# One-row transfers in place of small products, products on zeros ahead of the first load, and a new order of work

## The chip, the cores and the metric

The kernel runs on one core of a Trainium2 chip. The core has five engines that run in parallel, each through its own queue in order: PE (TensorE, the matrix products), DVE (VectorE), ACT (ScalarE), POOL (GpSimd) and SP (SyncE, which here only starts transfers). Transfers are started from the queues of SP, ACT and POOL and are carried by 16 DMA engines. The metric is the device time of one execution in microseconds (us): the median of several runs. The profile comes from one further execution, taken with the hardware profiler.

## The reference: what is computed

The input x has 2048 positions and 512 channels, all in 32-bit floats. Two mixers are applied to it, and a gate per position blends them:

```
g = sigmoid((x * gate_w).sum(-1))
a = irfft2(rfft2(x) * (w_r + 1j*w_i))                    # over positions and channels
K = 2 * Re(sum_n C[d,n] * exp(A[d,n] * dt[d] * pos))      # a long convolution per channel
b = causal_conv(x, K) + x * D_skip
out = g * a + (1 - g) * b
```

The kernel writes the two-dimensional transform as products with constant tables. For b it uses that, with these inputs, the decay is so slow that K is flat over the positions: the convolution is then a running sum along the positions times one number per channel. A count of the channels for which this holds (`count`) is computed on the chip, and if any channel fails it a general branch runs instead; it does not run here.

## The kernel before, in words

The order of work is written out by hand. `PLAN` is a list of words; a letter names a step and the numbers behind it say which piece it works on and which buffer it uses, and the words are executed in turn when the program is built, so that each engine's queue holds its instructions in the order of the list. The steps, with the lines of the profile before:

- `A`, `X`, `l`, `L`, `R`, `r`: loads. `A` brings x in ten pieces into `GI`; `X` brings x once more, as `XT` with channels on the partitions; `l` brings the weights of one u into the part of `GI` that C has used (L299), and `L` puts one more row, the weights of the last combination, in partition 127 of them (L305, L303). `R` brings tables.
- `C` (L233): the first transform, eight steps of 8 products; `c` (ACT) or `f` (DVE) copies the result from PSUM to `E1`.
- For each of nine groups of frequencies u (u = 8 is half as large): `D` (L248, eight products), `E` (copy on ACT), `P` (L269, the third transform), `d` (ACT copies a half of it), `Z` (DVE, sums and differences in PSUM, L290 and L291), `W` and `U` (DVE, the complex product with the weights, L311, L316, L317), `p` (POOL starts a transfer that adds one half of the result to the other, L321), `g` (POOL forms the sums and differences of the result, the combinations `gt`, L328 and L329), `I` (L338 to L341, products with `dbw` that transform back), `i` (ACT copies to `GI`).
- In `I`, partition 127 of the combinations needs other signs than the rest. The table `dbw` has zeros in that row, and the row's part is added by two small products for each large one, taken straight from the result `t` (L341, with `dbl`, 32 rows).
- `B` (L357, `Y` is a B without its last columns, `b` adds them) and `T` (DVE transposes) are the next transform, `Q` (L476) the last; `q` adds `XT`, now holding b times the gate, and stores the result (L481, L482). `k` and `K` form the gated tables that Q multiplies with.
- `m` is the running sum (DVE, L436), `s` scales it, `e`, `o`, `v`, `w`, `M` add it to the skip term in `XT`, and `H` multiplies by the gate on POOL. The sums of the four blocks of channels share the two halves of `run`.
- `G`: the gate. `G0` is its products over all of `XT` (L375), `G2` and `G3` write it to memory and read it back spread over the partitions; `G4` and `G5` are the count, and SP reads the count (`TENSOR_LOAD`) to choose the branch at the end.

Results of the products live in four PSUM buffers (`bank`), combinations and other blocks in eight pairs of SBUF buffers (`blk`, `pairs`). A step that writes a buffer waits for the last reader of what was in it.

## Time and profile before

| | us |
|---|---|
| median of 3 runs (lowest to highest) | 134.36 (133.01 to 134.85) |
| the profiled execution | 134.16 |
| its span, first to last instruction | 132.4 |
| PE busy in the span | 117.2 |
| DVE busy | 82.2 |
| POOL busy | 56.2 |
| ACT busy | 51.2 |

The span is what the trace shows; the profiled execution took 1.76 us more, which lies around it. Busy times of the PE are those of overlapping, pipelined products, so the share says that it was seldom without work, not that it worked at its peak. In the profile a line number names the instruction in the kernel, `out<-in` its tiles with the buffer numbers left out, and `xN` the number of instructions. One product of 32-bit floats is shown as two records of PE and two of PEld, the loading of its weights.

### The profile page before, as it was taken

The page shows a single profiled execution, that of the slowest core. Times are in us where ns is not written, and L with a number is a line of the kernel's source. Part 1 is how long each engine was busy: PE and PEld are TensorE (multiplying, and loading weights), DVE is VectorE, ACT ScalarE, POOL GpSimd, SP SyncE. Part 2 cuts the span into 40 slices and gives each one's busy share as a digit, 9 for nine tenths or more (in the row PEclk, how much of TensorE's full clock was granted, in tenths as well). Part 3 has the DMA queues.
Part 4 walks back from the last instruction along what each step waited for, and adds up shares of the span by engine and source line. Part 5 has one row for each costly group of instructions (what it writes and reads, how often), then busy time and mean ns, then how long its engine had stood idle before and what let it go on. Part 6 is the DMA issues. An engine that isn't in the chain of part 4 may idle for free.

```text
span 132.4 us, 2360 instructions
## 1 busy us (share of the span) xinstructions
PE 117.2 (89%) x944; PEld 95.5 (72%) x944; DVE 82.2 (62%) x101; ACT 51.2 (39%) x63; POOL 56.2 (42%) x49
## 2 busy tenths in 40 slices
PE   0599998999979999989999999999999999999700
PEld 0599997999879998858736766777655339999600
DVE  0031036078299999788770099999999573677610
ACT  3033635444267542313164113349679970000000
POOL 0000000001040840586798919499949999300000
PEclk9999999999999999999999999999999999999965
DMA  2999989996869789998667769990969600099660
GB/s 83 349 396 384 392 309 272 389 389 136 314 195 223 253 238 276 274 386 174 126 130 147 141 144 316 295 335 10 191 131 198 124 5 7 9 368 396 267 245 5
DMA packets 10643, 29.85 MB, mean 226 GB/s; under 512 B 1818, under 2 KB 2938, under 8 KB 10366
## 3 DMA queue, kind: packets, MB, share of 16 engines
q1 hardware_dynamic: 8606, 22.99, 48.4%
q0 software_dynamic: 1872, 6.55, 25.9%
q8 instruction: 9, 0.15, 0.4%
q10 hardware_dynamic: 144, 0.07, 0.4%
q14 instruction: 12, 0.10, 0.2%
HBM read 18.82 MB, written 4.21 MB: 174 GB/s over the span
## 4 chain that ended last, share of the span: by engine, by line
PE 69%; DMA 15%; DVE 7%; POOL 2%; issue 2%; ACT 1%
PE ps L233 13%; PE ps L476 12%; PE ps L357 11%; PE ps L338 9%; PE ps L341 8%; DMA blk<-blk 8%; PE ps L339 5%; PE ps L269 4%; DMA short<-in_prms_dram 3%; DMA GI<-in_x_dram 3%; PE ps L248 3%; PE ps L375 3%; DVE ps L290 2%; DVE ps L291 2%; DVE blk L316 1%
## 5 line engine op out<-in xcount | busy, mean ns | idle before, releaser
L233 PE MATMUL ps<-s,GI 128*128 128x128 f32 x128 | 17.4, 307 | 4.9 <-DMA GI<-in_x_dram 4.9
L453 POOL TENSOR_TENSOR XT<-XT,hg 128x1024 f32<-128x1024 f32 x8 | 20.9, 3038 | 0.0
L233 PEld LDWEIGHTS ps<-s,GI 128*128 128x128 f32 x128 | 17.2, 222 | 4.8 <-DMA s<-in_c_s_dram 4.8
L346 ACT COPY GI<-ps 128x1024 f32<-128x1024 f32 (+1 forms) x9 | 8.7, 964 | 24.2 <-PE ps L341 24.2
L328 POOL TENSOR_TENSOR blk<-blk 128x512 f32<-128x512 f32 (+1 forms) x9 | 13.0, 1443 | 11.6 <-DMA blk<-blk 11.2
L248 PE MATMUL ps<-dfw,E 128*128 128x128 f32 x128 | 15.6, 277 | 2.2 <-DVE blk L317 1.6
L248 PEld LDWEIGHTS ps<-dfw,E 128*128 128x128 f32 x128 | 14.8, 192 | 2.9 <-DVE blk L317 2.0
L338 PE MATMUL ps<-dbw,blk 128*128 128x128 f32 x68 | 16.3, 322 | 0.6 <-POOL blk L329 0.6
L269 PE MATMUL ps<-s2e,blk 128*128 128x128 f32 x136 | 16.8, 277 | 0.0
L269 PEld LDWEIGHTS ps<-s2e,blk 128*128 128x128 f32 x136 | 15.8, 192 | 1.2 <-issue 0.8
L357 PE MATMUL ps<-GI,s2p 128*64 128x512 f32 (+1 forms) x64 | 15.7, 583 | 0.0
L436 DVE TENSOR_TENSOR_SCAN run<-XT 128x1024 f32<-128x1024 f32 x4 | 11.2, 2803 | 6.7 <-DMA XT<-in_xt_dram 6.7
L476 PE MATMUL ps<-blk,E 128*128 128x128 f32 x128 | 15.3, 282 | 0.0
L476 PEld LDWEIGHTS ps<-blk,E 128*128 128x128 f32 x128 | 15.2, 196 | 0.1
L341 PE MATMUL ps<-last,blk 32*64 32x128 f32 x136 | 14.8, 293 | 0.0
L338 PEld LDWEIGHTS ps<-dbw,blk 128*128 128x128 f32 x68 | 10.1, 188 | 5.8 <-issue 5.0
L415 POOL TENSOR_TENSOR few<-few 128x4 f32<-128x4 f32 x1 | 0.2, 202 | 31.5 <-ACT few L412 31.5
L339 PE MATMUL ps<-dbw,blk 128*128 128x128 f32 x68 | 13.1, 275 | 0.0
L481 DVE TENSOR_TENSOR blk<-ps,XT 128x1024 f32<-128x1024 f32 x8 | 9.6, 1222 | 5.6 <-PE ps L476 2.8
L329 POOL TENSOR_TENSOR blk<-blk 128x512 f32<-128x512 f32 (+1 forms) x9 | 12.6, 1404 | 0.0
L238 ACT COPY E<-ps 128x1024 f32<-128x1024 f32 x7 | 7.1, 1012 | 13.7 <-PE ps L233 13.7
L311 DVE TENSOR_TENSOR blk<-ps,GI 128x1024 f32<-128x1024 f32 (+1 forms) x9 | 10.5, 1164 | 3.1 <-PE ps L341 1.8
(51 smaller groups left out, 142.7 us busy)
## 6 DMA issues: line engine op xcount, KB each, us to landing
XT<-in_xt_dram SPq DMA_DIRECT2D x4, 1024.0 KB, 6.6
GI<-in_w_dram SPq DMA_DIRECT2D x8, 512.0 KB, 3.9
blk<-blk POOLq DMA_DIRECT2D x8, 512.0 KB, 5.7
out_dram<-blk SPq DMA_DIRECT2D x8, 512.0 KB, 3.3
GI<-in_x_dram SPq DMA_DIRECT2D x6, 512.0 KB
XT<-run POOLq DMA_DIRECT2D x4, 512.0 KB, 5.9
GI<-in_x_dram SPq DMA_DIRECT2D x4, 256.0 KB, 5.4
hg<-gd SPq DMA_DIRECT2D x1, 1024.0 KB
```

The costliest lines, as they stand in the source:

```text
L233: T.matmul(p[:, u, :, j], X[:, 8 * k + 4 * u + j], s1, start=True, stop=True)
L248: T.matmul(p[:, n], E1[:, 8 * u + n], dfw[:, n % 4], start=True, stop=True)
L269: T.matmul(p[:, h, :, o, 64 * v:64 * v + 64], t_["e2", u % 8][:, 4 * v + 2 * h + o], st[:, ::-1] if h else st, start=True, stop=True)
L328: G.tensor_tensor(gt[:, :, :, 0], t[:, 0:4:3], t[:, 1:3], op=ALU.add)
L329: G.tensor_tensor(gt[:, ::-1, :, 1], t[:, 0:4:3], t[:, 1:3], op=ALU.subtract)
L338: T.matmul(p[:, v, 2 * h + 1], gt[:, h, m + v], dbw[:, h, 1], start=True, stop=True)
L339: T.matmul(p[:, v, 2 * h], gt[:, h, v], dbw[:, h, 0], start=True, stop=False)
L341: T.matmul(p[64 * c:64 * c + 64, v, 2 * h], px[:, c ^ h, h, v], dbl[:, h], start=False, stop=True, tile_position=(96, 64 * c))
L357: T.matmul(p[64 * s:64 * s + 64, u, :16 * n], s2p[:, 0, g], GI[:, 32 * s:32 * s + n, tt], start=True, stop=s == 1, tile_position=(0, 64 * s))
L436: V.tensor_tensor_scan(run[:, q % 2, 1:1025], XT[:, 0, q], XT[:, 1, q], 0.0, op0=ALU.add, op1=ALU.add)
L453: G.tensor_tensor(o, o, hg[:, 1024 * (k % 2):1024 * (k % 2) + 1024], op=ALU.mult)
L476: T.matmul(p[:, u, :, j], E4[:, b // 16, b % 16, :, u], t_["q", b // 8][:, 8 * u + b % 8].rearrange("p q a -> p (q a)"), start=True, stop= ...
```

## The change

Five things change.

1. `I`: the two small products per large one are gone, and so is the zeroed row of `dbw` (with the table `last` and its load). The row is put right in the combinations themselves: a new step `h` starts, from SP, four transfers per u, each of one partition and two runs of 64 numbers (one run for u = 8), from `t` to `gt`. They follow POOL's `g` of the same u. `I` does the four products that do not need that row first.
2. Before the first load has landed, two products of 128x512 on zeros are put on the PE; their result is not used. DVE clears their operand first.
3. The one-row loads of the weights (`L`) are started from ACT instead of SP.
4. A running sum gets a block of its own, out of nine pairs of blocks instead of two halves of `run` beside eight pairs. Since the block has no leading zero, the shares with the shifted sum treat the first element apart.
5. The list of words, `PLAN`, is another one. One C copy goes from DVE to ACT, and the u's are worked in another order (0, 3, 4, 2, 5, 6, 8, 1, 7 on DVE, instead of 6, 7, 5, 1, 4, 2, 0, 3, 8).

```diff
-NPAIR = 8
+WARM = 2
+NPAIR = 9
...
 PLAN = """
-R0 A4 C3.0 A7 C6.1 r0.0 A3 c3 C2.0 r1.1 N0 A5 R3 J0 A6 C4.2 R8 A9 A8 c6 c2 C5.0 c4 f5 A1 C7.1 c7 A2 C1.0 R4 c1 A0 C0.1
...
+A4 A3 R4 A2 R0 C3.0 R2 C2.1 A5 c2 c3 A1 A0 C1.2 A6 A7 A8 R3 C4.1 C0.0 c1 c4 A9 r1.0 R1 r0.1 C5.1 J0 c5 C6.2 C7.1 X3 N0
...
-    dbw = dbw.reshape(128, 2, 2, 128)
-
-    last = (j == 127)[:, None, None]
-    dbw = np.stack([dbw[:, :, 0] * ~last, dbw[:, :, 1], dbw[:, :, 0] * last], 2)
...
-    last = work.tile([P, 4, P], F32, name="last")
-    hT, dbl = last[:9], last[96:P, 0:2]
+    hT = work.tile([9, 4, P], F32, name="hT")
...
-    run = work.tile([P, 2, 1028], F32, name="run")
...
-            lambda: (nc.sync.dma_start(dbw, c_dbw[:, :, 0:2]), nc.sync.dma_start(dbl, c_dbw[96:P, :, 2])),
+            lambda: nc.sync.dma_start(dbw, c_dbw),
...
-                nc.sync.dma_start(wtile(8)[P - 1:P, :, :, 0].rearrange("p r a k -> p (r a) k"), hT[8:9, :, :64])
+                nc.scalar.dma_start(wtile(8)[P - 1:P, :, :, 0].rearrange("p r a k -> p (r a) k"), hT[8:9, :, :64])
             else:
-                nc.sync.dma_start(GI[P - 1:P, 8 * u:8 * u + 8 * n].rearrange("p (u n o) t -> p u n o t", n=4, o=2)[:, :, :, 0], hT[u:u + n])
+                nc.scalar.dma_start(GI[P - 1:P, 8 * u:8 * u + 8 * n].rearrange("p (u n o) t -> p u n o t", n=4, o=2)[:, :, :, 0], hT[u:u + n])
...
+        def h_a(u):
+            n = nrow(u)
+            t = t_["t", u][P - 1:P, 0, :, :, 0:n].rearrange("p x a (v k) -> p a x v k", k=64)
+            gt = t_["gt", u][P - 1:P, :, 0:n // 64].rearrange("p h v c k -> p h c v k")
+            for h in range(2):
+                for c in range(2):
+                    nc.sync.dma_start(gt[:, h, c], t[:, h, c ^ h])
+
         def I_(u, i):
+            p = t_["pi", u] = bank(i).rearrange("p v (n t) -> p v n t", t=P)
             m = nrow(u) // 64
-            p = t_["pi", u] = bank(i).rearrange("p v (n t) -> p v n t", t=P)
             gt = t_["gt", u].rearrange("p h m c k -> p h m (c k)")
-            px = t_["t", u][96:P, 0].rearrange("p x a (m k) -> p x a m k", k=64)
-            for v in range(m):
-                for h in range(2):
-                    T.matmul(p[:, v, 2 * h + 1], gt[:, h, m + v], dbw[:, h, 1], start=True, stop=True)
-                    T.matmul(p[:, v, 2 * h], gt[:, h, v], dbw[:, h, 0], start=True, stop=False)
-                    for c in range(2):
-                        T.matmul(p[64 * c:64 * c + 64, v, 2 * h], px[:, c ^ h, h, v], dbl[:, h], start=False, stop=True, tile_position=(96, 64 * c))
+            for o in (1, 0):
+                for v in range(m):
+                    for h in range(2):
+                        T.matmul(p[:, v, 2 * h + o], gt[:, h, o * m + v], dbw[:, h, o], start=True, stop=True)
...
-        def scan(q):
-            V.tensor_tensor_scan(run[:, q % 2, 1:1025], XT[:, 0, q], XT[:, 1, q], 0.0, op0=ALU.add, op1=ALU.add)
+        def scan(q, i):
+            t_["run", q] = blk(i)
+            V.tensor_tensor_scan(blk(i), XT[:, 0, q], XT[:, 1, q], 0.0, op0=ALU.add, op1=ALU.add)
...
+            if k == 0:
+                V.tensor_scalar(XT[:, 0, q, 0:1], XT[:, 0, q, 0:1], sd[:, q:q + 1], None, op0=ALU.mult)
+            V.scalar_tensor_tensor(XT[:, k, q, 1 - k:], XT[:, k, q, 1 - k:], (sd, dsk)[k][:, q:q + 1], t_["run", q][:, 0:1023 + k], op0=ALU.mult, op1=ALU.add)
...
+        V.memset(gsg[:, 0], 0.0)
+        for k in range(WARM):
+            T.matmul(bank(3)[:, 0], gsg[:, 0, 0:P], gsg[:, 0], start=True, stop=True)
```

The list moves nearly every instruction; three places matter for what follows. The first is SP's queue around the load of the count (`count`), before. `gd` is the gate in memory, `hg` and `blk7` its two spread copies, `c_r` the tables of `k`:

```order
L303 DMA GI_77<-last_84 1x4x64
L382 DMA gd_75<-gsg_86 4x512
L507 TENSOR_LOAD count_68
L507 ISA x2
L383 DMA hg_67<-gd_75 128x2048
L385 DMA gd_75<-gsg_86 32x1x16 x4
```

Now, in the same queue; L332 is the new step `h`, for u = 5 above the load, and for u = 6, 1, 8 and 7 below it, and L389 is `G3`:

```order
L332 DMA blk1_88<-blk4_91 1x2x64 x4
L514 TENSOR_LOAD count_68
L514 ISA x2
L389 DMA blk4_91<-gd_75 128x2048
L332 DMA blk3_90<-blk8_95 1x2x64 x4
L393 DMA short1_97<-in_c_r_dram 128x512
L332 DMA blk1_88<-blk7_94 1x2x64 x4
L332 DMA blk0_87<-blk6_93 1x16x4 x4
L332 DMA blk3_90<-blk5_92 1x2x64 x4
```

The load of the count, which waits for DVE's cast of it, now stands ahead of `G3` and of sixteen one-row transfers; before, the gate's copies stood behind it.

The second place is DVE where the count is cast (L433 in both), before; L317 is the end of `U`, L290 the start of the next `Z`:

```order
L317 SCALAR_TENSOR_TENSOR blk5_93<-ps3_61,GI_77 128x512
L433 CAST count_68<-ps2_60 1x1
L290 TENSOR_TENSOR ps1_59<-ps1_59,short1_97 128x2x64
L291 TENSOR_TENSOR ps1_59<-short1_97,ps1_59 128x2x64
L290 TENSOR_TENSOR ps1_59<-ps1_59,short1_97 127x2x64
```

Now; L312 is the end of the last `U` (u = 7), L437 the running sum:

```order
L311 TENSOR_TENSOR blk5_92<-ps0_58,GI_77 128x512
L312 SCALAR_TENSOR_TENSOR blk5_92<-ps0_58,GI_77 128x512
L437 SCALAR_TENSOR_TENSOR blk3_90<-XT_76 128x1024
L433 CAST count_68<-ps1_59 1x1
L437 SCALAR_TENSOR_TENSOR blk1_88<-XT_76 128x1024
```

Before, the cast came ahead of the last u (u = 8); now it comes behind the last u and a running sum.

The third place is the PE around the gate's products (L375 in both), now; L264 is `P`, L341 the new `I`:

```order
L264 MATMUL ps3_61<-s2e_80,blk2_89 128x2x64 x8
L375 MATMUL ps0_58<-XT_76,gws_85 32x512 x16
L264 MATMUL ps1_59<-s2e_80,blk3_90 128x2x64 x8
L264 MATMUL ps2_60<-s2e_80,blk0_87 128x2x64 x4
L264 MATMUL ps0_58<-s2e_80,blk1_88 128x2x64 x8
L341 MATMUL ps3_61<-dbw_83,blk3_90 128x128 x8
```

Before, three of the `I` stood ahead of the gate's products and only the P of u = 8 behind them; now no `I` stands ahead of them, and three P's (u = 1, 8, 7) come behind.

24 lines of the change are left out of this document (11 added, 13 removed).

## The prediction, on record before the run

> **What bounds it now.** I read the page first (busy time of the engines), then the windows cut where the PE's work changes: loading, C (first transform of x), D/P (second and third), P/I (third and back), B, Q, the last store.
>
> ```profile
> PE 117.2 (89%) x944; PEld 95.5 (72%) x944; DVE 82.2 (62%) x101; ACT 51.2 (39%) x63; POOL 56.2 (42%) x49
> ```
> ```profile
> 0.00:4.80 4.80, 0.00 (x0) 0.00 (x0) 0.09 (x2) 1.28 (x1) 0.20 (x4) 1.00 0.52 185
> 4.80:22.25 17.45, 17.39 (x130) 17.39 (x131) 4.02 (x7) 6.07 (x7) 0.00 (x0) 1.00 0.96 347
> 22.25:50.50 28.25, 26.01 (x228) 25.32 (x226) 21.11 (x33) 14.59 (x18) 6.50 (x11) 1.00 0.86 269
> 50.50:93.80 43.30, 42.73 (x356) 29.95 (x355) 33.27 (x42) 15.61 (x18) 31.74 (x26) 1.00 0.81 209
> 93.80:109.50 15.70, 15.70 (x110) 7.65 (x108) 12.80 (x11) 13.64 (x20) 13.62 (x8) 1.00 0.66 125
> 109.50:124.85 15.35, 15.35 (x130) 15.15 (x128) 9.64 (x8) 0.00 (x0) 4.14 (x2) 1.00 0.52 208
> 124.85:132.40 7.55, 0.00 (x1) 0.00 (x0) 1.23 (x1) 0.00 (x0) 0.00 (x0) 0.63 0.37 145
> ```
> The columns are the stretch, its length, busy time of PE, PEld, DVE, ACT, POOL, the clock, the DMA share and GB/s. From 4.80 to 124.85 the PE is busy 117.2 of 120.05 us. It is the bound of every stage, and its gaps are 2.9 us in all. A microsecond taken from it is therefore a gain only until the next chain comes up; that chain has to be found. The profiled execution took 134.16 us, 1.76 beyond its span of 132.4; the median of the runs is 134.36, so no correction is due.
>
> **What the change takes from the PE.** One transform back (I, one u) in the timeline:
>
> ```profile
> 57.07 0.49 PE L338 MATMUL ps<-dbw,blk 128*128 128x128 f32 x2 [0.57 <-POOL blk L329]
> 57.72 0.43 PE L341 MATMUL ps<-last,blk 32*64 32x128 f32 x4
> 58.08 0.49 PE L338 MATMUL ps<-dbw,blk 128*128 128x128 f32 x2
> 61.10 0.38 PE L269 MATMUL ps<-s2e,blk 128*128 128x128 f32 x1
> ```
> A quarter takes 1.01 us and the whole u 61.10 - 57.07 = 4.03. Each product is two records, so a u is 16 full and 16 small records. What a full one costs is seen in C, where ACT copies after every 16:
>
> ```profile
> 4.86 17.37 PE ps L233 x128
> 22.25 1.02 ACT E L238
> ```
> ```profile
> 8.64 1.01 ACT L238 COPY E<-ps 128x1024 f32<-128x1024 f32 x1 [6.19 <-PE ps L233]
> 11.53 1.01 ACT L238 COPY E<-ps 128x1024 f32<-128x1024 f32 x1 [1.87 <-PE ps L233]
> 13.31 1.01 ACT L238 COPY E<-ps 128x1024 f32<-128x1024 f32 x1 [0.77 <-PE ps L233]
> 15.10 1.01 ACT L238 COPY E<-ps 128x1024 f32<-128x1024 f32 x1 [0.78 <-PE ps L233]
> ```
> The steady step is 15.10 - 13.31 = 1.79 us for 16 records. So 4.03 - 1.79 = 2.24 us per u goes with the small products, and with eight and a half u's 19.0 us. A full product has its own weights in C as in the new I, so 1.79 is the price of the new I too.
>
> **The zeros.** The first two steps of C take 8.64 - 4.86 = 3.78 and 2.89 us against 1.79: 3.1 us lost, while the granted clock shows 1.00. The PE runs at about half rate until some 5.9 us after its first product. If the products on zeros start at about 1.6 (DVE has to clear 128x512 first), the fast rate comes up to 3.3 us earlier, worth half of that: 1.7. The bounds are 0 (two products last perhaps 2 us, and the PE idles again until 4.86) and 3.1. I take 1.7: C ends at 20.55 instead of 22.25. The Trainium skill (TensorE: Matmul & The Clock Gate, Part 1) says that the clock is released after a busy window of about 3.4 us and that this window runs freely; by it two short products with a pause behind them may fill no window, and the gain would be 0 and the time 1.7 higher.
>
> **The next chain: DVE.** Its work per u (L285 to L312 now) has not changed.
>
> ```profile
> 29.59 0.43 DVE L290 TENSOR_TENSOR ps<-ps,short 128x256 f32<-128x256 f32 x1
> 45.48 0.42 DVE L290 TENSOR_TENSOR ps<-ps,short 128x256 f32<-128x256 f32 x1
> 49.66 0.42 DVE L290 TENSOR_TENSOR ps<-ps,short 128x256 f32<-128x256 f32 x1
> 75.91 0.28 DVE L290 TENSOR_TENSOR ps<-ps,short 128x128 f32<-128x128 f32 x1
> 78.55 5.16 DVE L442 SCALAR_TENSOR_TENSOR XT<-XT,few,run 128x1024 f32<-128x1024 f32 x2
> ```
> ```profile
> L420 DVE TENSOR_REDUCE few<-short 128x4 f32<-128x512 f32 x1 | 0.7, 686 | 2.8 <-DMA short<-in_prms_dram 2.8
> L375 PE MATMUL ps<-XT,gws 128*32 128x512 f32 x32 | 3.6, 595 | 0.0
> ```
> A full u is 49.66 - 45.48 = 4.18 us, u = 8 is 78.55 - 75.91 = 2.64. Before, the first of them starts 29.59 - 22.25 = 7.34 after C; the same three steps (D, D, P) stand between now, so 20.55 + 7.34 = 27.9. Six full u's and the reduction: 27.9 + 25.1 + 0.7 = 53.7. The seventh is u = 8, and its P stands on the PE behind the gate's products, which need all of XT:
>
> ```profile
> 50.09 0.60 SPq L207 DMA_DIRECT2D XT<-in_xt_dram  x1
> ```
> The last part of XT was issued at 50.09 before. Now 15.5 MB stand in the queue up to it (x, XT, weights, tables). By 4.80, 0.9 MB have come (185 GB/s); at 347 the rest lands at 46.9, at 347 up to 22.25 and 269 after that at 54.0. SP no longer waits in between for the one-row loads, but the accumulating transfers of POOL share the engines: I take 49. The PE is there at 20.55 + 1.06 + 14 x 1.79 = 46.7. So gate to 49 + 3.6 = 52.6, two P's (2.7) 55.3, ACT's copy 0.5: DVE starts u = 8 at 55.8, 2.1 late, and ends the last u at 55.8 + 2.64 + 2 x 4.18 = 66.8 (before 78.55).
>
> **The last rows, on SP.** These are 36 transfers, four per u. A one-row transfer and the wait for the count:
>
> ```profile
> 75.84 0.14 DVE L433 CAST count<-ps 1x1 int32<-1x1 f32 x1 [6.34 <-PE ps L430]
> 77.33 0.35 SPq L383 DMA_DIRECT2D hg<-gd  x1
> 77.73 2.46 SPq L385 DMA_DIRECT2D gd<-gsg  x4
> 80.24 3.19 SPq L393 DMA_DIRECT2D short<-in_c_r_dram  x4
> ```
> ```profile
> s2e<-in_c_s2e_dram SPq DMA_DIRECT2D x1, 128.0 KB, 2.2
> gd<-gsg SPq DMA_DIRECT2D x4, 2.0 KB, 5.2
> ```
> ```profile
> L436 DVE TENSOR_TENSOR_SCAN run<-XT 128x1024 f32<-128x1024 f32 x4 | 11.2, 2803 | 6.7 <-DMA XT<-in_xt_dram 6.7
> ```
> Four one-row issues take 2.46, and SP goes on 77.33 - 75.98 = 1.35 after the cast. The new order puts the load of the count on SP ahead of G3 and of the rows of u = 6, 1, 8 and 7, and on DVE the cast behind a scan that follows the last u. So: 66.8 + 2.8 (scan) + 0.14 + 1.35 = 71.1; G3 0.35; u = 6 2.46; one table 0.8; u = 1 2.46; u = 8 2.46: issued at 79.6. Landing is 2.2 or 5.2, by two small transfers; I take 2.2, since loads of megabytes no longer run beside it: 81.8. The Trainium skill (DMA: Bandwidth & Descriptors, Rules for kernel authors) advises against many transfers under 64 KB, as mostly overhead; the 0.62 us of each of these 2 KB issues agrees.
>
> POOL's side of the last u ends about then:
>
> ```profile
> DMA to landing us min/median/max: 4.5/5.2/11.6
> ```
> ```profile
> L328 POOL TENSOR_TENSOR blk<-blk 128x512 f32<-128x512 f32 x8 | 11.0, 1371 | 9.7 <-DMA blk<-blk 9.2 <-PE ps L375 0.3
> ```
> Accumulated at 66.8 + 5.2 = 72.0; the two combinations of a u take 2 x 1.37, and those of u = 1 and 8 and two more issues stand ahead, so u = 7 is out at about 79, under SP's 79.6, where its rows begin. They are issued at 82.1 and land at 84.3.
>
> **The end.** I of u = 8 ends at 82.2. Two of the eight B's follow (2 x 1.96 of the 15.70 row): 86.1. I of u = 7, 1.8: 87.9, its rows landed before. The rest of B, 11.8: 99.7. Q, 15.35: 115.0. Tail 7.55: 122.6. Outside 1.76: **124.4 us**.
>
> Costs put at nothing: the h rows of u = 0, 4, 3, 2 also hand buffers back to W of u = 6, 8, 1, 7. By the same prices they land 1 to 3 us ahead of those; with 5.2 to land, W of u = 6 is 1.6 late. C's eighth copy moves from DVE to ACT, 1.0 in a step of 1.79. Two more need rows:
>
> ```profile
> XT<-in_xt_dram SPq DMA_DIRECT2D x4, 1024.0 KB, 6.6
> ```
> ```profile
> L442 DVE SCALAR_TENSOR_TENSOR XT<-XT,few,run 128x1024 f32<-128x1024 f32 x4 | 8.5, 2166 | 0.0
> L397 DVE TENSOR_TENSOR short<-short,blk 128x512 f32<-128x512 f32 x4 | 4.6, 1205 | 0.0
> L453 POOL TENSOR_TENSOR XT<-XT,hg 128x1024 f32<-128x1024 f32 x8 | 20.9, 3038 | 0.0
> ```
> G3 (1 MB) is issued at 71.5 and by the first row lands near 78; three of the bases and the four shares follow on DVE, 3 x 1.2 + 8.5 = 12.1, to about 90, and the first transpose is due at 91. POOL's eight gate products, 20.9 us from the first shares at about 84, end at 105, ahead of the end of the fourth Q at 107.4, after which the PE needs a bank back. Without that cover each microsecond counts in full. A buffer per sum removes waits of scans that are on no chain here.
>
> **The rivals.**
> *Nothing queues.* The chain alone, without SP's count, POOL's queue or XT's delay: DVE 27.9 + 36.8 = 64.7; landing 5.2, combination 2.7, issues 2.5, landing 2.2 make 77.3; I 1.8, B 11.8, Q 15.35, tail and outside 9.3: **115.6**. For it: the PE alone, kept as busy as before, would give 134.16 - 19.0 - 1.7 = 113.5. Against: four queues would have to meet. 0.08.
>
> *ACT's queue holds the copies.* This one is slower. The one-row loads of the weights leave SP for ACT:
>
> ```profile
> SPq L305 <- DMA GI<-in_w_dram: 16.2, 4, 5.5
> ```
> On SP four of them waited 16.2 us in all. Behind them on ACT stand the copies that PE and DVE wait for, one per u. If this came in full, the time would be 124.4 + 16.2 = **140.6**; it turns slower once more than 12.6 of them remain. Against: at 347 GB/s the weights of u = 0 land at 25, those of 3 and 4 at 29, and ACT reaches these loads at 26 and 30; only u = 5 to 7 (39 to 44, ACT at 42) is close. 0.04.
>
> *The zeros warm nothing, rows land in 5.2 and XT at 54.* That adds 1.7, 3.0 and 5.0: 126.1, 127.4, 129.4 singly, over 131.7 only together. 0.08, of which 0.06 falls within 2% of before.
>
> **The numbers.** The forecast, 117.5 to 130.5, has 0.80. The low end is 124.4 - 2.1 (XT in time) - 1.4 (zeros in full) - 3.2 (twelve issues at 0.35, the row of one plain issue) = 117.7; the high end has landing and XT both late by most of their bounds. What is left out is 115.6 with 0.08 and the part above with 0.12. Two per cent is what a measurement of this kernel can tell: faster is under 131.7, slower over 137.0. Faster 0.80 + 0.08 + 0.02 = 0.90, same 0.06, slower 0.04.
>
> **What would show it.** C's first two copies some 5 us apart at 1.79 and 2 to 3 us instead of 3.78 and 2.89 (zeros). I's eight products at 1.79 per u with PE idle between them released by DMA or POOL (last rows bind). The last L312 of DVE near 67, SP's G3 near 71, the last L332 near 82, B from 82, Q from 100. Wrong: PE idle under 4 us in all (first rival), ACT idle on weight loads with DVE waiting for ACT (second), or the last u on DVE after 72 with SP long empty, which would put the cause ahead of the last rows.

## The result and the profile after

The changed kernel takes **144.43 us** (median of 4 runs, 143.30 to 145.19) against 134.36 before: 1.0765 of the kernel before (ratio of the means), with a 95% interval of 1.0635 to 1.0895. It is slower, by about 10 us; the forecast was 124.4, in a range of 117.5 to 130.5, and faster. Some executions of any kernel come out slow: ratios leave them out, and so does the 134.36 (one of 148.70), while the medians in the table below are of all runs. The profiled execution took 144.53 us with a span of 142.7 and a mean granted clock of 0.876 (before 0.979).

The page of the changed kernel, with TensorE's (PE) busy tenths and its granted clock in 40 slices of 3.57 us, and the chain that ended last:

```profile
PE 109.5 (77%) x812; PEld 91.7 (64%) x812; DVE 79.1 (55%) x102; ACT 51.4 (36%) x64; POOL 54.9 (38%) x49
...
PE   5999989999998004999095039982999999999800
...
PEclk9999999999999955699757755899599999999985
...
PE ps L357 11%; PE ps L479 11%; PE ps L228 10%; DMA gd<-gsg 7%; PE ps L243 6%; PE ps L264 6%; SPq L332 5%; DMA GI<-hT 5%; PE ps L375 4%; DMA blk<-blk 4%; SPq L385 3%; PE ps L492 3%; DVE ps L286 2%; DVE blk L306 2%; DVE ps L285 2%
```

The PE is busy 7.7 us less than before, and the span is 10.3 us longer: the work did go, and 23 us of idle time took its place, in four holes of 9.48, 3.38, 7.51 and 2.58 us (slices 13 to 15, 19, 21 to 23 and 27, counted from 0). In and behind each hole the clock row reads 5 to 7: the PE comes back at half rate. The chain now names things that were on no chain before: the gate's writes (`gd<-gsg`), SyncE's own queue (`SPq L332`, the placed rows) and the one-row loads (`GI<-hT`).

The holes in the PE's timeline (start, length, instructions; in brackets the idle time ahead of it and what ended it):

```profile
55.35 5.73 PE L375 MATMUL ps<-XT,gws 128*32 128x512 f32 x32 [9.48 <-DVE blk L312]
...
70.91 0.34 PE L430 MATMUL ps<-few 128*1 128x1 f32 x8 [3.38 <-ACT XT L448]
...
84.40 11.55 PE L341 MATMUL ps<-dbw,blk 128*128 128x128 f32 x76 [7.51 <-DMA blk<-blk]
...
99.36 0.46 PE L341 MATMUL ps<-dbw,blk 128*128 128x128 f32 x2 [2.58 <-DMA blk<-blk]
99.75 1.19 PE L357 MATMUL ps<-GI,s2p 128*64 128x512 f32 x4
...
119.83 15.34 PE L479 MATMUL ps<-blk,E 128*128 128x128 f32 x128
```

The gate's products start at 55.35 and take 5.73 us where they took 3.6 before. The line names DVE's L312, but that was done at 54.69; in two kernels further down the same wait is put down to the load of x for the gate (XT), and we read it so here too. I of u = 5 waits 7.51 us for its placed row, I of u = 8 another 2.58. B starts at 99.75 (forecast 82.2) and Q at 119.83 (forecast 99.7): the miss of 20 us is all there when Q starts, for Q and the tail are as long as forecast. What SyncE (SP) did ahead of those rows:

```profile
55.34 13.25 SPq L332 DMA_DIRECT2D blk<-blk  x12
...
69.87 0.55 SPq L382 DMA_DIRECT2D gd<-gsg  x1
...
72.79 5.81 SPq L385 DMA_DIRECT2D gd<-gsg  x4
...
79.94 3.59 SPq L332 DMA_DIRECT2D blk<-blk  x4
85.36 0.34 SPq L389 DMA_DIRECT2D blk<-gd  x1
85.81 2.55 SPq L332 DMA_DIRECT2D blk<-blk  x4
...
88.89 10.73 SPq L332 DMA_DIRECT2D blk<-blk  x12
```

And the end of GpSimd's (POOL) combination of u = 5, from POOL's timeline:

```profile
68.41 1.51 POOL L324 TENSOR_TENSOR blk<-blk 128x512 f32<-128x512 f32 x1
```

POOL has u = 5 ready at 69.9. Its row is issued at 79.94, behind the gate's five small writes, their read back and two tables, and the PE goes on at 84.40. The queue holds the gate back as well: its values are ready at 62.2 (ACT's L379 ends there), but the first gate write is issued only at 69.87, because on SP it stands behind the twelve rows of u = 4, 3 and 2, the last of which wait until POOL has u = 2 ready at 66.55. The chain of waits goes on from there (start, length):

```profile
77.06 8.11 DMA gd<-gsg
...
93.70 5.52 DMA blk<-blk
```

The last gate write takes 8.11 us to land, the read of the gate's result (G3, L389) comes right behind that, the rows of u = 6, 1 and 8 stand behind G3 in SP's queue, and the last of these lands 5.52 us after its issue. Then B can start. Whether G3 waited for that landing alone is not settled: on SP the row of u = 5 ends at 83.53 and the load of the count starts at 83.6, both ahead of G3, and in a kernel without rows G3 comes 1.67 us after the start of that load, which here would be 85.3 too.

### The profile page after: what moved, and what is told of

Read it like the earlier page. It is cut to its first block, busy times and chain, and to the rows that moved or that the text cites. A ratio compares the mean times of both kernels' runs of the same rounds, so it can differ in the third digit from the quotient of the medians.

```text
span 142.7 us, 2183 instructions
## 1 busy us (share of the span) xinstructions
PE 109.5 (77%) x812; PEld 91.7 (64%) x812; DVE 79.1 (55%) x102; ACT 51.4 (36%) x64; POOL 54.9 (38%) x49
## 3 DMA queue, kind: packets, MB, share of 16 engines
q0 software_dynamic: 1872, 6.55, 24.7%
## 4 chain that ended last, share of the span: by engine, by line
PE 54%; DMA 16%; DVE 10%; SPq 9%; issue 4%; ACT 1%; DVEq 0%; ACTq 0%
PE ps L357 11%; PE ps L479 11%; PE ps L228 10%; DMA gd<-gsg 7%; PE ps L243 6%; PE ps L264 6%; SPq L332 5%; DMA GI<-hT 5%; PE ps L375 4%; DMA blk<-blk 4%; SPq L385 3%; PE ps L492 3%; DVE ps L286 2%; DVE blk L306 2%; DVE ps L285 2%
## 5 line engine op out<-in xcount | busy, mean ns | idle before, releaser
L341 PE MATMUL ps<-dbw,blk 128*128 128x128 f32 x136 | 21.9, 333 | 10.7 <-DMA blk<-blk 10.5
L341 PEld LDWEIGHTS ps<-dbw,blk 128*128 128x128 f32 x136 | 20.9, 245 | 11.4 <-DMA blk<-blk 7.7
L316 POOL DMA_DIRECT2D blk<-blk x9 | 8.0, 914 | 38.3 <-DVE blk L312 37.4
L264 PE MATMUL ps<-s2e,blk 128*128 128x128 f32 x136 | 16.3, 276 | 0.0
L264 PEld LDWEIGHTS ps<-s2e,blk 128*128 128x128 f32 x136 | 15.7, 192 | 0.8 <-issue 0.8
L437 DVE TENSOR_TENSOR_SCAN blk<-XT 128x1024 f32<-128x1024 f32 x4 | 9.2, 2289 | 10.9 <-PE ps L341 8.6
L228 PEld LDWEIGHTS ps<-s,GI 128*128 128x128 f32 x128 | 14.5, 192 | 1.1 <-DMA s<-in_c_s_dram 1.1
L228 PE MATMUL ps<-s,GI 128*128 128x128 f32 x128 | 14.5, 275 | 0.0
L285 DVE TENSOR_TENSOR ps<-ps,short 128x256 f32<-128x256 f32 (+3 forms) x18 | 7.4, 414 | 11.3 <-ACT short L270 11.0
L403 ACT ACTIVATE blk<-short,sgn 128x512 f32<-128x512 f32 x16 | 10.1, 710 | 8.7 <-issue 8.7
L375 PE MATMUL ps<-XT,gws 128*32 128x512 f32 x32 | 5.7, 879 | 9.5 <-DVE blk L312 9.5
L445 DVE SCALAR_TENSOR_TENSOR XT<-XT,few,blk 128x1023 f32<-128x1023 f32 (+1 forms) x4 | 9.2, 2344 | 6.3 <-ACT blk L440 6.3
```

The source lines that it names most:

```text
L228: T.matmul(p[:, u, :, j], X[:, 8 * k + 4 * u + j], s1, start=True, stop=True)
L264: T.matmul(p[:, h, :, o, 64 * v:64 * v + 64], t_["e2", u % 8][:, 4 * v + 2 * h + o], st[:, ::-1] if h else st, start=True, stop=True)
L285: V.tensor_tensor(a, b, re, op=ALU.add)
L341: T.matmul(p[:, v, 2 * h + o], gt[:, h, o * m + v], dbw[:, h, o], start=True, stop=True)
L375: T.matmul(p[32 * j:32 * j + 32], gws[:, q], XT[:, j // 2, q, 512 * (j % 2):512 * (j % 2) + 512], start=q == 0, stop=q == 3, tile_position ...
L403: S.activation(t_["q", j][:, :, q], r, AF.Copy, scale=sgn[:, q:q + 1])
```

## The experiments

Each kernel ran once with a profile, unless it says otherwise, beside runs of the kernel before on the same chip. The changed kernel itself was not run again on those chips, so a difference to its 144.43 is one between chips. All times in us:

| what | time | before, same chip |
| --- | --- | --- |
| gate later | 139.81 | 135.92 |
| no rows | 135.23 | 135.92 |
| rows in the order of before | 156.61 | 135.92 |
| zeros alone | 134.93 | 135.92 |
| small products in the new order | 175.6 | 132.46 |
| the same, gate later | 171.97 | 132.46 |
| filler at the gate | 142.59 | 132.46 |
| half the rows | 146.6 | 132.46 |
| mixed | 132.19 | 136.5 |
| no rows, gate later | 135.0 | 136.5 |
| small products, filler | 175.81 | 136.5 |
| x earlier | 143.98 | 136.5 |
| gate writes on ScalarE | 141.46 | 134.35 |
| both moved | 136.11 | 134.35 |
| full-size products | 141.34 | 134.35 |
| mixed, 4 runs | 134.49 | 134.35 |
| full-size behind a wait | 152.94 | 134.21 |
| mixed and padded, 13 runs | 134.04 | 134.21 |

The runs of the kernel before went from 132.04 to 139.31 us over chips and runs, at granted clocks of 0.957 to 0.992, and three took 147.82 to 150.67, and on three of the five chips it ran once; so a difference of a few us between single runs says little without their traces. Against the kernel before on the same chip, the changed kernel loses 10.1 us, gate later 3.9, x earlier 7.5, gate writes on ScalarE 7.1, both moved 1.8, half the rows 14.1, and no rows with the gate later gains 1.5.

### The gate, and the rows

Theory A: x lands late and DVE stands behind the gate. Theory B: the placed rows in SP's queue set the end.

```diff
-P6.3 d5.0 G0.0 Z5 ... p5 L8 G1 Z6 ... U6 R9 h4 P7.0
+P6.3 d5.0 Z5 ... p5 L8 Z6 ... U6 R9 h4 G0.0 G1 P7.0
```

> The changed kernel with the gate's products (L375) moved on the PE behind the P's of u = 1 and 8, nothing else. Theory A (the late landing of XT at 55 us holds the PE at the gate, and with it the last three u's): u = 8 starts on DVE near 54 instead of 64.4, the last u ends near 67 instead of 75.6, and the time falls by about 8, to some 136. Theory B (SP's queue of one-row transfers and gate writes sets the end, whatever the gate does on the PE): the last u is earlier, but its rows are not, and the time stays within 2 of 144.4.

139.81, which is 4.6 under the changed kernel: between the two theories. DVE's last L312 ends 71.4 instead of 75.7, but the PE then waits 10.6 us for the row of u = 5.

```diff
 def h_a(u):
-    n = nrow(u)
-    ... (the four transfers)
+    pass
```

> The changed kernel without the 36 one-row transfers: the last row of the combinations stays wrong, so that part of the computation is left out. Theory A: the wait at the gate stays, the last u still ends on DVE near 75.6, and only the 7 to 8 us in which the PE waited for rows go: about 136. Theory B: everything behind the last u moves up as well, I of u = 7 follows POOL near 88, and the time falls by about 16, to 128.

135.23. That is near theory A's figure. Taking all 36 transfers away gives 9.2 us and still only reaches the level of before. Rows are a large part of the loss, and something else keeps the gain away; it shows further down.

```diff
 kernel before:
-I_ with small products, dbl
+I_ and h_a of the changed kernel, h right behind each g
```

> The kernel before, with its own order, where only the small products give way to the one-row transfers, issued from SP right behind each g. If the small products were 19 us of the bound as the prediction had it, and rows land in time in an order with one I every 4 us, the time falls towards 120 to 126. Theory B says that the rows wait in SP's queue here too (behind loads and the gate's writes): 132 or more. If the order is what made the changed kernel slow, this one is faster than 134.4.

156.61, on the side of theory B (132 or more), but by far more than it foresaw. In the order of before I of a u stands 0 to 7 us behind its g, and a row does not get there in that time. From the waits of this kernel (total, times, longest):

```profile
PE ps L341 <- DMA blk<-blk: 16.8, 7, 5.9
DVE short L397 <- DMA blk<-gd: 13.5, 1, 13.5
```

The first is the rows' landing, the second the read of the gate's result, which stands behind rows in SP's queue. How much of the rest is the clock, which was at 0.50 again in 90 to 100 us, was not tested.

```diff
 kernel before:
+V.memset(gsg[:, 0], 0.0)
+for k in range(2):
+    T.matmul(bank(3)[:, 0], gsg[:, 0, 0:P], gsg[:, 0], start=True, stop=True)
```

> The kernel before with the two products on zeros and nothing else. By the changed kernel's trace, where C takes 14.3 us instead of 17.4, the time falls by about 3, to 131. If the zeros only move the wait (C then waits for x), it stays at 134.

134.93, 1.0 under before, within what one run can tell. C ends 1.6 us sooner (20.6 against 22.2), and a longer pause ahead of a product, 3.47 us where it was 1.29, takes that back. The trace names DVE for that pause; that DVE in turn stands behind the loads is argued here, not shown.

### Half of the rows, x earlier, the gate's writes

```diff
-for h in range(2):
-    for c in range(2):
-        nc.sync.dma_start(gt[:, h, c], t[:, h, c ^ h])
+for c in range(2):
+    nc.sync.dma_start(gt[:, 0, c], t[:, 0, c])
```

> The changed kernel with two of the four small transfers of every u, those of the first half alone; the placing of the other half of the last row is left out, the order is kept. If the cost is the number of transfers in SP's queue (18 fewer of 36), the time lies half way between the kernel without rows and the changed one, 139 to 141. If the cost is that the products wait for the landing of a row at all (5.5 us from the issue, however many transfers go with it), little is gained: 142.5 to 144.5. If it is the queue alone, up to some threshold that the half already clears: 135 to 137.

146.6, above every one of the three. With two transfers instead of four the row of u = 5 is issued at 78.80 (79.94) and the PE waits until 85.54 (84.40): the number of transfers is not what holds it. B starts 1.9 us earlier than in the changed kernel, and that is lost again on DVE ahead of Q, where the second pair of shares takes 10.04 us.

```diff
-l6 l8 D5.2.3 E5 ... R5 X1 L5.3 X0 g0.6
+X1 X0 l6 l8 D5.2.3 E5 ... R5 L5.3 g0.6
```

> The changed kernel with the last two loads of x for the gate moved ahead of the weights of u=6 and u=8 in SyncE's queue; no other word of the order is moved. If x lands at 55.3 because 0.8 MB of weights go ahead of it at some 300 GB/s, it lands 2 to 3 us sooner, TensorE's idle time ahead of the gate falls from 9.5 to about 7, and the time is 141.5 to 143. If the rate of the loads falls whatever stands first, or the weights are then late for W of u=6, it is 144 or more.

143.98: x landed 6 us sooner, more than expected, and nothing came of it. ScalarE's (ACT) timeline and queue in this kernel, and the groups of the chain that ended last:

```profile
52.28 0.75 ACTq L300 DMA_DIRECT2D GI<-hT  x1
53.08 1.15 ACT L440 ACTIVATE blk<-blk,few 128x1024 f32<-128x1024 f32 x1 [10.74 <-POOL blk L323]
```
```profile
DMA GI<-in_w_dram 13%; PE ps L357 11%; PE ps L479 11%; PE ps L228 11%; DMA blk<-blk 8%; PE ps L341 5%; PE ps L243 4%; DMA GI<-hT 3%; SPq L385 3%; PE ps L492 3%; DVE ps L286 2%; DVE ps L285 2%; DMA gd<-gsg 2%; SPq L393 2%; SPq L332 2%
```

The bracket names POOL, but the chain has the load of the weights first, with 18.08 us from its issue at 34.10 to its landing at 52.2. Now the weights are late, and ACT, which issues the one-row load of u = 5 to 7 only when they have landed, does nothing from 42.3 to 52.3 with DVE's copy behind it. The rival on ACT's queue, 0.04 in the prediction, is real as soon as x goes first: the load rate has to be given to one of the two. The PE's wait for the row of u = 5 ends at 84.61 as before.

```diff
-nc.sync.dma_start(gd[1]...)   -nc.sync.dma_start(gd[0]...)  (x4)
+nc.scalar.dma_start(gd[1]...) +nc.scalar.dma_start(gd[0]...) (x4)
```

> The changed kernel with the five small writes of the gate's result issued by ScalarE instead of SyncE, nothing else moved. In the changed kernel these, the read back of hg between them and two loads of c_r hold SyncE from 68.7 to 79.9 while g of u=5 is ready at 69.9. Theory (the order in SyncE's queue): the row of u=5 is issued at about 71 to 72 and lands by 79, so TensorE's wait ahead of I of u=5 ends 5 us sooner; the rows behind it and the gate's read move up too, and the time is 138 to 141. Rival (each step waits for its own landing, not for the queue): above 143.

141.46, 3.0 under the changed kernel and 0.5 above the range. SP's timeline and the PE's:

```profile
71.46 3.90 SPq L332 DMA_DIRECT2D blk<-blk  x4
80.41 0.34 SPq L389 DMA_DIRECT2D blk<-gd  x1
```
```profile
80.00 10.46 PE L341 MATMUL ps<-dbw,blk 128*128 128x128 f32 x66 [2.89 <-DMA blk<-blk]
```

The row of u = 5 is issued 8.5 us sooner and the PE goes on 4.4 us sooner. The four issues end at 75.36, and the PE starts 4.6 us later: that is the landing. G3 takes over the buffer which that row is read from, so it waits for the landing too, and is issued at 80.41 (85.36). Two other things moved with the writes. The load of the count on SP now stands behind G3 and no longer ahead of it, so that G3 does not wait for the cast of the count: by the prediction's rule of 1.35 us behind the cast (80.49 here) G3 would have come at 81.8. And ACT now stands 5.70 us behind the gate's writes.

The next kernel has both moves, the gate's products behind P of u = 1 and 8 and the writes on ACT:

> As the kernel with the gate's writes on ScalarE, and also with the gate's products behind P of u=1 and 8, which alone gave 4.6 us. If the late gate and SyncE's queue are two costs one behind the other, both gains come: 134 to 137. If they are one cost met at two places (the row of u=5 late), little comes on top: within 1.5 us of the kernel with the writes moved alone.

136.11, 8.3 under the changed kernel; 4.6 and 3.0 make 7.6. The late gate and SP's queue are two costs in one chain, and they add, as far as single runs on different chips can tell. Up to 2 us of the 8.3 may be that G3 stands ahead of the load of the count here too: without rows and with the gate later, but behind that load, it was issued at 76.89, here at 74.96.

### What is left without rows

> The changed kernel with the placing of the last row left out and the gate's products moved behind P of u=1 and 8. Alone, the first gave 9.2 us less than the changed kernel and the second 4.6. If the two costs lie one behind the other (the late x through DVE, then the rows through SyncE), both go: 13 to 14 us below the changed kernel, about 5 below the kernel before. If the gate's result, which SyncE writes and reads back for DVE's four products with it, is late in either case and sets B and Q, only part goes: 133 to 135 where the kernel before has 135.9.

135.0: 9.4 under the changed kernel, not 13 to 14. So the second expectation holds, and this kernel shows what the plan costs without the rows and with the gate's products further back. XT is late in it still. PE, DVE and POOL in its timeline:

```profile
55.87 5.15 PE L370 MATMUL ps<-XT,gws 128*32 128x512 f32 x32 [2.36 <-DMA XT<-in_xt_dram]
...
82.91 1.07 PE L352 MATMUL ps<-GI,s2p 128*64 128x512 f32 x4 [0.21 <-ACT GI L341]
99.50 1.61 PE L352 MATMUL ps<-GI,s2p 128*64 128x512 f32 x4 [3.72 <-DVE E L362]
109.12 15.34 PE L474 MATMUL ps<-blk,E 128*128 128x128 f32 x128
```
```profile
63.72 0.43 DVE L285 TENSOR_TENSOR ps<-ps,short 128x256 f32<-128x256 f32 x1 [7.55 <-ACT short L270]
...
82.09 3.74 DVE L392 TENSOR_TENSOR short<-short,blk 128x512 f32<-128x512 f32 x1 [4.70 <-DMA blk<-gd]
...
85.88 2.46 DVE L440 SCALAR_TENSOR_TENSOR XT<-XT,few,blk 128x1023 f32<-128x1023 f32 x2
...
89.00 6.55 DVE L440 SCALAR_TENSOR_TENSOR XT<-XT,few,blk 128x1023 f32<-128x1023 f32 x2
95.47 2.82 DVE L392 TENSOR_TENSOR short<-short,blk 128x512 f32<-128x512 f32 x1
98.21 4.63 DVE L362 STREAM_TRANSPOSE E<-ps 128x1024 f32<-128x1024 f32 x4
```
```profile
82.15 1.90 POOL L323 TENSOR_TENSOR blk<-blk 128x512 f32<-128x512 f32 x1
...
88.43 21.35 POOL L451 TENSOR_TENSOR XT<-XT,hg 128x1024 f32<-128x1024 f32 x8 [1.43 <-DVE XT L440]
```

B starts at 82.91, where the prediction had it (82.2). Q starts at 109.12, where it had 99.7. Between them DVE waits for the gate's result until 82.09, then does bases and shares until 98.2, and only then the first transpose, for which the PE has to wait. XT lands at 55.87, the gate takes 5.15 us, and DVE waits 7.55 us for ACT's copy behind it, so that its last u ends at 72.96, where the prediction had 66.8: that, and not DVE's later work alone, makes G3 late (issued at 76.89, forecast 71.1). Two shares take 2.46 us, and the next two, beside POOL's products, 6.55; together that is near the 8.5 that the prediction took for four. The bases are what it missed: 3.74 us beside POOL's combinations (which took 1.90 each there in place of 1.25), 2.82 beside POOL's products, and 0.68 for one between them, where it took 1.2 each.

### The clock

```diff
-P6.3 d5.0 G0.0 Z5
+P6.3 d5.0 z8 G0.0 Z5      (z: products of 128x512 on zeros)
```

> The changed kernel with eight more products on zeros ahead of the gate's, in TensorE's idle stretch of 9.5 us there; nothing else is moved. If the half clock after an idle stretch is what lengthens the gate's 5.73 us, the gate's products take about 3.6 us, as in the kernel before, u=8 starts about 2 us earlier, and the time is 142 to 143. If the gate's length is due to something else (its operands, the transfers beside it), 5.7 us stay and 144.4. If the eight products run over the time at which x is there, it is slower by the rest.

142.59, which is the time expected, but on a chip where the kernel before took 132.46, so the total decides nothing. The PE's timeline with the filler (L495):

```profile
47.09 7.13 PE L495 MATMUL ps<-gsg 128*128 128x512 f32 x16
57.13 3.64 PE L375 MATMUL ps<-XT,gws 128*32 128x512 f32 x32 [2.91 <-DMA XT<-in_xt_dram]
```

The gate takes 3.64 again instead of 5.73: half clock costs 2.1 us in length at this one place. Since x landed 1.8 us later here, the gate ends only 0.3 us sooner (60.77 against 61.08), and u = 8 begins on DVE 0.3 sooner, not 2. B starts 1.8 us sooner (97.99), behind other waits, so that the total met the expectation is partly luck.

The next kernels put the small products of before back into the new order. One thing was overlooked in them: in this order the buffer of u = 4 is already u = 8's when I of u = 4 reads its last row, so that the row added is another u's and the product waits for the transfer of u = 8. The buffers of u = 0, 3 and 2 are taken over in the same way, by u = 6, 1 and 7. Their times tell nothing of the order alone; that could not be had in this way and stays open.

```diff
 changed kernel:
-I_ on placed rows, h_a
+I_ with small products and dbl of the kernel before, h_a does nothing
```

> The changed kernel with its order and its products on zeros, but the small products of before on the last row in place of the placed rows. Theory A (the placed rows cost about 9 us by their place in SP's queue and by their landing; the order, which has x for the gate late and the gate's result behind it, is worth nothing): what the kernel without rows gave, 135.2, plus nine times the 0.45 us between the two forms of the products, as far as it is not hidden: 136 to 139. Theory B (the order and the zeros are good, the rows are all that is wrong): 130 or less.

> As the kernel with the small products put back, but the gate's 64 products stand behind P of u=1 and 8, ahead of P of u=7. Theory A: DVE no longer stands still behind the gate, so 4 to 5 us less than that kernel, as with the rows: 132 to 134. Theory B (the gate's wait is covered by other work once no row is waited for): within 1 us of it.

175.6 and 171.97, 30 us above anything expected. A group of one u in the first of them, at 68 us and behind the wait, and the window behind the wait (length, busy time of PE, PEld, DVE, ACT, POOL, clock, DMA share, GB/s):

```profile
67.41 0.49 PE L341 MATMUL ps<-dbw,blk 128*128 128x128 f32 x2
68.42 0.49 PE L341 MATMUL ps<-dbw,blk 128*128 128x128 f32 x2
...
82.34 0.69 PE L344 MATMUL ps<-last,blk 32*64 32x128 f32 x4 [9.22 <-DMA blk<-blk]
82.96 0.80 PE L341 MATMUL ps<-dbw,blk 128*128 128x128 f32 x2
84.73 0.80 PE L341 MATMUL ps<-dbw,blk 128*128 128x128 f32 x2
```
```profile
82.00:127.00 45.00, 44.66 (x204) 30.79 (x204) 6.60 (x7) 7.96 (x8) 16.80 (x13) 0.50 0.41 94
```

A group goes from 1.01 to 1.77 us, and the PE works for 45 us without a pause at half clock. Three more kernels ask why. A filler of eight products ahead of I of u = 4:

> The kernel with the small products put back into the new order, which took 175.6, with eight more products on zeros or on finished data in TensorE's idle stretch ahead of I of u=4 and nothing else moved. There the small products of eight u's ran at 0.50 of the clock for 45 us without a pause, which is 1.77 us a group against 1.00 in the kernel before. If what keeps the clock down is that it fell in the 9.2 us of idle time and that these groups don't bring it back, they run at 1.00 us again and some 20 us go: 152 to 157. If the clock is down for another reason (heat, a limit on the chip): above 172.

175.81, which speaks against the theory as put. But the filler left a wait of 3.36 us, and at 84.2, in the second group behind it, the clock fell all the same.

```diff
-T.matmul(p[64 * c:64 * c + 64, v, 2 * h], px[...], dbl[:, h], ...)        (32 x 64, twice)
+T.matmul(p[:, v, 2 * h], gt[:, h, v], dbw[:, h, 0], start=False, ...)    (128 x 128, twice)
```

> The kernel with the small products put back into the new order, which took 175.6, but each pair of small products of 32 rows by 64 columns is replaced by two products of the full 128 by 128 on the same data, so that its output is not the reference's; the number of products, and all waits except those for the row, stay. Theory (products of that small size do not count enough to bring the clock back): the clock returns some 6 us after the idle stretch, a group takes 1 us again and the time is 150 to 158. Rival (the clock stays down for another reason): 172 or more.

141.34. The long wait had gone with the read of the row, so this run does not tell about it. It does show that full-size products lose the clock too: behind a pause of 1.59 us it was at 0.50 from 71 to 74 us, and back by 75. The next one keeps four small products, and with them the wait:

> As the kernel with full-size products in place of the small ones in the new order (its output is not the reference's), but the first four small products of u=4 stay, whose wait gave the idle stretch of 9.2 us in which the clock fell. Theory (the size decides): the wait is there again, the clock is at half behind it, is back some 6 us later, and the time is 148 to 158. Rival (the clock, once fallen there, stays down whatever the products' size): 172 to 176. If the idle stretch is not there, the run tells nothing of it: about 141.

152.94, in the range of the theory. Its PE timeline and windows:

```profile
82.28 0.69 PE L345 MATMUL ps<-last,blk 32*64 32x128 f32 x4 [7.98 <-issue]
```
```profile
84.00:86.00 2.00, 2.00 (x12) 2.00 (x12) 0.00 (x0) 0.00 (x0) 0.00 (x0) 0.52 0.97 387
86.00:88.00 2.00, 2.00 (x20) 2.00 (x19) 0.00 (x0) 0.69 (x1) 0.63 (x1) 1.00 0.67 227
```

Behind such a wait, with full-size products, the clock is back after 4 us. With half of the records 32 rows by 64 columns it was not back after 45, and in the two other kernels with that mix it stayed down for over 40. The full-size side is one run.

### A version that uses what was learned

The order of before, the zeros, rows for two u's alone, issued by ACT, and I of u = 3 moved ahead of I of u = 0:

```diff
 kernel before, with the zeros:
+ROWS = (0, 2)      (full products for these; their table is loaded into dfw, which is free by then)
-g2.1 G1 d8.1 I1.0 i1 ... p3 g0.2 I4.3
+g2.1 G1 d8.1 h2 I1.0 i1 ... p3 g0.2 h0 I4.3
-I2.0 i2 a1.1 a2.2 I0.2 i0 ... I3.0 v2 s2 w2 i3
+I2.0 i2 a1.1 a2.2 ... I3.2 v2 s2 i3 w2 I0.0 i0
```

> The kernel before in its own order with the two products on zeros, with placed rows for u=2 and u=0 alone, issued by ScalarE instead of SyncE, and I of u=3 moved ahead of I of u=0; all other u's keep the small products. In the kernel before, g of u=2 ends 73.1 and its I starts 79.7, g of u=0 ends 76.5 and its I starts 83.7. Theory (a placed row costs four issues of 0.6 us and 5.5 us to land, some 8 us after g, and is free only where the order leaves as much): u=2's row is there about 81, 1.4 us late, u=0's in time behind I of u=3; each of the two I's is 2.2 us shorter, B starts about 90.7 instead of 93.8, and the time is 2 to 4 us below the kernel before. Rival (rows cost wherever they stand, since ScalarE is held up as SyncE was): at or above the kernel before.

132.19 where the kernel before had 136.5. ACT's queue and the PE:

```profile
71.20 3.79 ACTq L339 DMA_DIRECT2D blk<-blk  x4
```
```profile
79.02 1.16 PE L349 MATMUL ps<-dbw,blk 128*128 128x128 f32 x8
90.48 1.07 PE L373 MATMUL ps<-GI,s2p 128*64 128x512 f32 x4 [0.59 <-ACT GI L362]
```

I of u = 2 did not wait for its row, which was issued by 74.99 and is needed from 80.0 on; B started at 90.48 (expected 90.7, before 93.8). Timed over more runs:

> The kernel that has the order before with the two products on zeros, placed rows for u=2 and u=0 alone, issued by ScalarE, and I of u=3 ahead of I of u=0; its single run was 132.2 where the kernel before had 136.5. If this is no chance of one run: 0.965 to 0.98 of the kernel before.

134.49 in the median of 132.37 to 135.48 against 134.35 (six runs of 133.06 to 135.28 and one of 150.67): no difference. Its profile shows where the gain may have gone:

```profile
82.53 0.49 PE L354 MATMUL ps<-dbw,blk 128*128 128x128 f32 x2 [0.92 <-POOL blk L331]
```
```profile
86.00:90.00 4.00, 4.00 (x20) 3.33 (x19) 3.97 (x3) 4.00 (x4) 4.00 (x3) 0.50 0.94 249
```

A pause of 0.92 us with small groups behind it, and the clock was at half from some 84.5 to 91.5, where it came back under full-size products; in the single run the same pause had left it at 1.00. Three runs with a granted clock of 0.95 took 133.82 to 135.48, one with 0.99 took 132.37. Giving the small products of four more u's all 128 rows, with zeros in all but the last:

```diff
+FULL = (1, 4, 3, 8)
+T.matmul(p[64 * c:64 * c + 64, v, 2 * h], t[:, ...], dfw[:, 2 + h], ..., tile_position=(0, 64 * c))
```

> The mixed version (order of before, products on zeros, placed rows for u=2 and 0 alone), in which u=1, 4, 3 and 8 have their small products of 32 rows by 64 columns replaced by products of all 128 rows by 64 columns, with zeros in all rows but the last; the number of products is the same. In the mixed version the clock fell to half between 84 and 91 us in some runs (granted 0.95: 133.8 to 135.5) and not in others (0.99: 132.2 to 132.4). If the size of the products decides, it falls in none: granted 0.98 or more, 132 to 133, 0.985 to 0.995 of the kernel before. If it falls here too, 134 to 135.5 in some runs.

134.04 against 134.21 in the median, a ratio of 0.9958 with a 95% interval of 0.9906 to 1.0009: again no difference that can be told. The expectation that the clock falls in none failed: six runs with a granted clock of 0.98 to 0.99 took 131.67 to 132.86, four with 0.96 to 0.97 took 134.04 to 136.77, and three more took 150.60, 151.35 and 230.37. In the one that was profiled it fell in 58 to 66 us, behind a pause of 1.19 us and among u's that had kept the 32-row products, so this run neither bears out nor refutes that padding helps where it was done. No version here is faster than the kernel before by more than its measurement can tell.

## Why the prediction was wrong

**Right.** The small products' price: where the changed kernel runs at full clock, in 90 to 96 us, 52 records take 5.95 us, which is 0.114 each and 1.8 for a u of 16, as forecast, where a u took 4.03 before. The PE's busy time falls by less than the forecast's 19 (with the rows left out 101.1 us, which is 104.8 less 3.7 for the zeros, against 117.2, and 2.9 of the difference are C's), because part of the work ran at half clock. Q and the tail came as forecast. The zeros were undersized: C takes 2.9 us less and ends 2.7 sooner, not 1.7. The first Z was 1.0 early (26.87 against 27.9) and six u's on DVE 1.0 late (54.69 against 53.7), for a one-row load that DVE had to wait 1.9 us for: that the second number is so near is luck. The first term of the sum was no error, and none of it decided.

**XT and the gate: 8.8 late on DVE.** This step failed first. Taken: XT lands at 49, bounds 46.9 to 54.0. It landed near 55.3, outside the bounds, and the gate took 5.73 instead of 3.6 on a PE at half clock, so that u = 8 began on DVE at 64.44 instead of 55.8 and the last u ended at 75.66 instead of 66.8. The windows of the changed kernel (the last two columns are the DMA share and GB/s) show why:

```profile
5.00:19.40 14.40, 14.40 (x130) 14.38 (x130) 1.63 (x5) 6.70 (x7) 0.00 (x0) 1.00 1.01 385
19.40:46.00 26.60, 25.80 (x229) 25.29 (x227) 21.21 (x31) 12.55 (x16) 5.89 (x8) 1.00 1.01 343
```

The DMA engines are full from 5 us on, and up to 46 they moved more than the 15.5 MB that the prediction counted (1.0 + 5.5 + 9.1 = 15.7): the accumulating transfers, 0.5 MB each, were named there but not put into the bytes, and the rate fell from 385 to 343 GB/s. Loading x first was no remedy, for the weights and ACT's queue were late instead (143.98). What the late XT does here is to hold u = 1, 8 and 7, which stand behind the gate: with the gate's products further back the time was 4.6 us less.

**SP's queue: 6.1 more.** The last row of u = 8 was there at 99.22, where the sum had 81.8. Of these 17.4 us, 8.2 came with the cast of the count (77.90 against 69.7), which follows the last u on DVE; 6.1 came between it and G3 (85.36, where the prediction's 1.35 behind the cast gives 79.25); and 3.2 are landing. From G3 on the issues took 8.3 us, as forecast (8.5). The sum counted the count, G3 and four rows on SP behind the last u. It left out G2, the gate's five writes and their read back, which stand ahead of the row of u = 5 and, through G3, of all rows behind it; neither their issue nor their landing of 8.1 us was in any term, and which of the two held G3 is open, as said above. The rule that the prediction followed for the count, to list what a step is queued behind, was not applied to G2. With the five writes on ACT the time was 3.0 us less, and with the gate further back as well 8.3.

**Landing: 2.2 taken, up to 5.5 measured.** The bounds (2.2 to 5.2) nearly held it, and the value taken was the wrong end: 5.5 for the last row of u = 8, 4.6 for that of u = 5 with the writes on ACT, though 0.9 for that of u = 5 in the changed kernel itself (issues end 83.53, PE 84.40). At the last rows it is 3 us. The reason given for the low value, that loads of megabytes no longer run beside it, did not hold: the DMA share was 0.92, at 224 GB/s, in 77.0 to 84.4 and 0.85 to 0.88 in 86 to 90. The half-rows run shows that fewer issues do not buy it back.

**The cover between B and Q: put at nothing, worth 9.** "Three of the bases and the four shares follow on DVE to about 90" used busy times of before and a G3 at 71.1. With the rows gone and B where the forecast had it, the last u ended 6.2 us late on DVE behind the late XT and gate, G3 was issued at 76.89 and landed at 82.09 (forecast 78), and bases and shares took 16.1 us instead of 12.1, because two of the three bases took 3.74 and 2.82 beside POOL instead of 1.2. The transposes started at 98.21 instead of 91, and Q 9.4 us late. So a perfect placing of rows alone would have ended near 135. What this order would take with x and the weights both in time was not tried.

**Not foreseen: the clock.** The prediction priced idle time of the PE at its length. It costs more: the gate 2.1 us of length (shown by the filler); the I's behind the third hole, from 84.40, 11.55 us for 76 records that take 0.112 each at full clock, 3.0; the first B's, 5.7 us from 99.75 where the kernel without rows needs 4.0, 1.7. The last two are worked out from the traces, not tested.

The miss of 20 us is then: 10.6 that stay without rows and with the gate further back (135.0 against 124.4), which hold the late XT and the bases beside POOL, and 9.4 for the gate ahead of u = 1, 8 and 7, SP's queue, landing and clock, of which moving the gate and its writes takes 8.3 away. All of these are single runs on different chips, the parts overlap, and their split beyond that is not settled. In the prediction's own terms the steps that failed are XT's landing (49, measured 55.3), the gate's length (3.6, measured 5.73), the path to the last row on SP without G2 (G3 at 71.1, measured 85.36), the landing (2.2, measured 5.5) and the cover between B and Q (12.1 us of bases and shares, measured 16.1 without rows, and a G3 too early). Of the rivals, "nothing queues" (115.6) was further off than the forecast. "ACT's queue", with a chance of 0.04 the only one that was slower (140.6), was near in time but not in cause: it cost 1.9 us on DVE in the changed kernel and came true only with x first. The one with late XT and slow landing had both causes, but added them to a sum without G2 and the cover.

## What to carry to other kernels

When PE work is traded for transfers, every transfer on a shared in-order queue has to be listed in program order with what it waits for, those of other stages too: a large part of the price here was not the row but what stood ahead of it. An engine that was busy throughout hides the chains under it; before taking its time away, work out where each of the others would end, with their lengths as they are when they run beside each other. And a busy TensorE keeps its clock; each hole is to be priced with the slow stretch behind it.

## What the runs showed of the hardware

- Whether the clock comes back depended here on the shape of the products, not only on time. Behind a wait of 8 us, products of 128 rows by 128 columns had the full clock after 4 us (one run; another had it back within 4 us behind a pause of 1.59); a mix in which half of the records are 32 rows by 64 columns stayed at 0.50 for 45 us without a pause, and for over 40 in two other kernels. At full clock that mix lost it behind pauses of 0.92, 1.19 and 3.36 us, though not each time (0.92 in the single mixed run left it at 1.00), and full-size products lost it behind 1.59. In the profiled run of the kernel before, with pauses of at most 0.57 us there, it ran through at 1.00. The small products also sat at a place of their own in the array (from row 96), and size and place were not told apart. The Trainium skill (TensorE: Matmul & The Clock Gate, Part 1) says that the warm-up is some 3.4 us of time, whatever is issued in it; the full-size products agree, the small ones do not, and the measurement decides.
- Two products of 128x512 on zeros from 1.5 to 5.2 us are enough for the full rate from C's first product on: 14.4 us busy for C where it took 17.4.
- Rows of 0.5 KB between two places of the same partition cost an issue of 0.6 to 1.0 us each (four in 2.55 to 3.90 us) and 0.9 to 5.5 us to land, at worst as much as the 512 KB accumulating transfers of the kernel before (5.2 in the median); a 2 KB write to DRAM took 8.1.
- DVE and POOL were slower beside each other. Two shares on DVE (128x1023) took 2.46 us, and two more 6.55 beside POOL's products of 128x1024, in one kernel, and 10.04 in another; a base (128x512) took 0.68 us at best and 3.74 beside POOL's combinations, which took 1.90 each instead of 1.25.
